# Block-sparse attention with an ELU feed-forward, one core: keys, queries and x turned on TensorE in float32, keys and rows of v in natural order, more weights loaded ahead

## The chip, the core and the metric

The kernel runs on one core of a Trainium2 chip. The core has five engines, each with its own in-order instruction queue: TensorE (PE, with its weight loads as PEld), VectorE (DVE), ScalarE (ACT), GpSimd (POOL) and SyncE (SP, which here issues DMAs). PSUM holds what TensorE writes; the other engines read it from there. The metric is the device time of one execution in microseconds. One execution was also taken with the hardware profiler, and all lines of a profile come from such an execution.

## The reference

Two parts run one after the other. Float32 q and k, v of shape (4 batches, 8 heads, 768 tokens, 64); float64 weights `w_in` (512 x 2048) and `w_out` (2048 x 512). The sequence of a batch is 24 blocks of 32 tokens.

```python
scores = scale * np.matmul(q, k.transpose(0, 1, 3, 2))
mask = np.abs(blk_i - blk_j) <= 1                       # window of three blocks
mask = mask | (blk_i == 0) | (blk_j == 0) | (blk_i == n_blocks - 1) | (blk_j == n_blocks - 1)
...                                                     # and 3 sampled key blocks per query block
scores = np.where(mask, scores, -1000000000.0)
attn = softmax(scores)                                  # max subtracted, sum + 1e-9
x = np.matmul(attn, v)        # then (4, 8, 768, 64) -> (3072 tokens, 512)
h = x @ w_in
g = np.where(h > 0.0, h, np.exp(np.minimum(h, 0.0)) - 1.0)
out = g @ w_out
```

A query block of the middle sees eight key blocks: its window of three, the first and the last, and three sampled ones. The first and the last query block see all keys.

## The kernel before, in words

**Numbers.** TensorE multiplies float16. Each float32 operand is split into a high part (ScalarE casts with a scale, `hi_part`) and a low part (VectorE subtracts, `lo_part`), and each product is three matmuls: high-high, high-low, low-high. The float64 weights are read as bits: 32 pieces of 512 KB, each made into float32 by ScalarE, VectorE and GpSimd (`w_bits1`, `w_sign`, `w_bits2`) and split (`w_split`, its low part on GpSimd at L272). The loads go through three rooms `wk`.

**Chunks.** The 22 middle blocks of a batch make five units of four blocks (128 queries) and a half unit `UL` of the last two middle blocks. With unit 5 go the first and the last block as "special" queries over all keys (the functions `sp_...`). Two units are a chunk of 256 tokens; there are twelve chunks, three per batch, the order in batch 0 being (0,1), (4,5), (2,3), later (4,5), (0,1), (2,3). The feed-forward of a chunk is 8 times `ffn_h` (192 matmuls in all, L729), the ELU on ScalarE, VectorE and GpSimd (`ffn_act1` to `ffn_act5`, L737 to L754), and 96 matmuls of `ffn_o` (L764).

**Attention of a unit**, for four heads at a time (`qd` is 0 or 1): `scores` (L534) into PSUM, softmax in float32 (`sm_min`, L545, `sm_exp`, L560), split of p (`sm_hi`, `sm_lo`, L567 and L572), a transposing DMA of p issued by SP (`sm_T`, L579), the product with v (`attn_v`, L592), and `norm` (L612). The normalised x is split on ScalarE and GpSimd (`x_hi` L619, `x_lo` L623) and turned by a transposing DMA on SP (`x_T`, L628, for unit 5 L634).

**q, k, v.** `load_kv` and `load_q` load to two staging rooms (tag "st", `NST`), SP issues. q and k are split there, high part on ScalarE (L316), low part on VectorE (L319), and turned by transposing DMAs on SP (`prep_qT` L343, `prep_kT` L366). The keys lie in `kT` with even and odd tokens apart (a block is two runs of 16), so that a window that crosses a group of 256 tokens needs two matmuls. v is split to `vN` and stored to scratch rows in DRAM (`store_v`, L449); from there come, into two tiles `vg0` and `vg1` (one for each unit of a chunk), the windows (`gather_v`, L481, two to four DMAs on SP for a block), the first and last block (`edge_v`), and the sampled blocks (one indirect DMA of GpSimd for a block, L482). The sampled keys are copied on VectorE (`gather_k`, L493).

**The first chunk** is another: batch 0's keys, queries, p and x of chunk 0 are turned on TensorE in float32 by an identity matrix (`early_k` L383, `early_q`, `early_pT` L403, `early_x` L413), four transposes to a PSUM tile, then split out of PSUM.

**Order.** Each function is put at a step with a rank (`st.at`), and the functions are run in that order. A chunk's feed-forward takes 16 steps, its attention starts `LEAD` = 22 steps before it. From this a scheduler makes the order of each engine's queue; the queues are in order, so an instruction that waits holds back all that stand behind it on its engine. Pools with a number of buffers (`NBIG`, `NT`, `NE`, `NST`) set how far loads and exponentials may run ahead.

Of the kernel before, what the change touches and what calls it, by code (L numbers as in the profile page):

```python
# [7 lines left out]
F32 = mybir.dt.float32  # L8
# [6 lines left out]
BLOCK = 32  # L15
# [23 lines left out]
def kernel(  # L39
# [35 lines left out]
    HB = BLOCK // 2  # L75
# [60 lines left out]
    def build_index():  # L136

        pk = const.tile([1, NB, 1 + NR], I32, tag="pk", name="pk")
        n = all_[0:1, :, :, 0]
        nc.vector.tensor_scalar(  # L140
            pk[:, :, 1:], n, 3, 6, op0=ALU.logical_shift_right, op1=ALU.logical_shift_left)
        nc.vector.scalar_tensor_tensor(
            pk[:, :, 1:], n, GB - 1, pk[:, :, 1:], op0=ALU.bitwise_and, op1=ALU.bitwise_or)
        nc.vector.tensor_scalar(
            pk[:, :, 0], pk[:, :, 1], 4, None, op0=ALU.logical_shift_left)
        for r in range(1, NR):
            nc.vector.scalar_tensor_tensor(
                pk[:, :, 0], pk[:, :, 1 + r], 4 + 8 * r, pk[:, :, 0],
                op0=ALU.logical_shift_left, op1=ALU.bitwise_or)
        reg[0] = pk  # L150

        pm = const.tile([P, 2], I32, tag="pm", name="pm")
        p0, p1 = pm[:, 0:1], pm[:, 1:2]
        nc.gpsimd.iota(p0, pattern=[[0, 1]], base=0, channel_multiplier=1)
        nc.vector.tensor_scalar(
            p1, p0, HB, 3, op0=ALU.bitwise_and, op1=ALU.logical_shift_left)
        nc.vector.tensor_scalar(p0, p0, HB - 1, None, op0=ALU.bitwise_and)
        nc.vector.tensor_tensor(p0, p0, p1, op=ALU.bitwise_or)
        for r in range(NR):
            ps = slice(32 * r, 32 * r + 32)  # L160
            x, n = rix[ps], all_[ps, :, r, 0]
            nc.vector.tensor_scalar(
                x, n, 3, 8, op0=ALU.logical_shift_right, op1=ALU.logical_shift_left)
            nc.vector.tensor_tensor(x, x, p0[ps].to_broadcast([32, NB]), op=ALU.bitwise_or)
            nc.vector.tensor_scalar(
                n, n, GB - 1, 4, op0=ALU.bitwise_and, op1=ALU.logical_shift_left)
# [166 lines left out]
    def prep_q_hi(b, u):
        n = q_parts(nat_tile(("q", b, u)))
        hi_part(n[:, 0], q_in(stg["q", b, u]), QS)

    def prep_q_lo(b, u):
        n = q_parts(nat["q", b, u])
        lo_part(n[:, 1], q_in(stg.pop(("q", b, u))), n[:, 0], QS)

    def prep_qT(b, u):
        qT[b, u] = work.tile([P, 2 * NPAIR, P], F16, tag="qT", name=f"qT{b}_{u}")
        nc.sync.dma_start_transpose(qT[b, u], nat.pop(("q", b, u)))  # L343

# [3 lines left out]
    def k_parts(n):  # L348

        return n.rearrange("p (c l h d) -> p l h c d", c=2, l=2, h=4)  # L350

    def prep_k_hi(b, g, qd):
        n = k_parts(nat_tile(("k", b, g, qd)))
        hi_part(n[:, 0], kv_in(stg["k", b, g, qd]), KS)

    def prep_k_lo(b, g, qd):
        n = k_parts(nat["k", b, g, qd])
        s = kv_in(stg.pop(("k", b, g, qd)))
        for c in range(2):
            lo_part(n[:, 1, :, c], s[:, :, c], n[:, 0, :, c], KS)  # L360

    def prep_kT(b, g, qd):

        if b not in kT:
            kT[b] = work.tile([P, NQ, NG, 8, P], F16, tag="kT", name=f"kT{b}")
        nc.sync.dma_start_transpose(kT[b][:, qd, g], nat.pop(("k", b, g, qd)))  # L366
# [8 lines left out]
    def early_k(g, qd):
        if 0 not in kT:
            kT[0] = work.tile([P, NQ, NG, 8, P], F16, tag="kT", name="kT0")
        s = spare(1, 2 * g, 2).rearrange("p (c x) -> p c x", c=2)
        ps = ps_f.tile([P, 2, 2, P], F32, tag="f", name=f"kt{g}_{qd}")
        for c in range(2):  # L380
            for pp in range(2):
                x = (2 * qd + pp) * P
                nc.tensor.transpose(ps[:, c, pp, :], s[:, c, x : x + P], ident)  # L383
        y = kT[0][:, qd, g].rearrange("p (c l pp) i -> p l c (pp i)", c=2, l=2)
        ps = ps.rearrange("p c pp i -> p c (pp i)")
        hi_part(y[:, 0], ps, KS)
        lo_part(y[:, 1], ps, y[:, 0], KS)

    def early_q(b, u):
        s = stg.pop(("q", b, u))  # L390
        ps = ps_f.tile([P, NPAIR, P], F32, tag="f", name=f"qt{b}_{u}")
        for pp in range(NPAIR):
            nc.tensor.transpose(ps[:, pp, :], s[:, pp * P : (pp + 1) * P], ident)
        qT[b, u] = work.tile([P, 2 * NPAIR, P], F16, tag="qT", name=f"qT{b}_{u}")
        y = qT[b, u].rearrange("p (a l) i -> p l a i", l=2)
        hi_part(y[:, 0], ps, QS)
        lo_part(y[:, 1], ps, y[:, 0], QS)

    def early_pT(b, u, qd):
# [5 lines left out]
        hi_part(y[:, 0:8], ps, PS)  # L405
        lo_part(y[:, 8:16], ps, y[:, 0:8], PS)
        pT[b, u, qd] = y

    def early_x(b, u, t, c0):
        x, s = chunk_x(t), xf.pop((b, u))  # L410
        ps = ps_s.tile([P, NPAIR, P], F32, tag="s", name=f"xt{b}_{u}")
        for cc in range(NCC):
            nc.tensor.transpose(ps[:, cc, :], s[:, cc * P : (cc + 1) * P], ident)  # L413
        cs = slice(c0, c0 + P)
        hi_part(x[:, 0, :, cs], ps, 1.0)
        lo_part(x[:, 1, :, cs], ps, x[:, 0, :, cs], 1.0)

    def keys(b, js, qd, y, k0, n):

        g, j = divmod(k0, GB)  # L420
        t = kT[b][js, qd, g].rearrange("p (c y) i -> p c y i", c=2)
        return t[:, :, y, HB * j : HB * (j + n)]

    def ends_of_k(b):

        t = work.tile([P, NQ, 4, 2, 2, HB], F16, tag="kE", bufs=1, name=f"kE{b}")
        kE[b] = t
        for e, (g, j) in enumerate(((0, 0), (NG - 1, GB - 1))):
            for qd in range(NQ):
                nc.vector.tensor_copy(  # L430
                    t[:, qd, :, e].rearrange("p y c i -> p c y i"),
                    kT[b][:, qd, g, :, HB * j : HB * j + HB].rearrange(
                        "p (c y) i -> p c y i", c=2))
# [545 lines left out]
```

## Time and profile before

| | |
|---|---|
| median of 3 runs | 880.42 us (877.14 to 887.3) |
| profiled execution | 891.87 us, its span 890.1 us |
| mean granted TensorE clock | 0.883 |
| instructions in the span | 35171 |
| DMA | 132.40 MB, mean 149 GB/s |
| GpSimd L754 (`ffn_act5`) | 114.8 us, 96 instructions |
| TensorE L729 (high part of `w_in`) | 280.9 us, 1536 matmuls |
| TensorE L764 (high part of `w_out`) | 244.1 us, 768 matmuls |

The busy shares of the engines stand in the prediction. A share is a mean over the span: it doesn't say where an engine is the bound. In a row `x22 | 24.6, 1120 | 20.6 <-ACT xn L619 20.3` the group has 22 instructions that took 24.6 us in all and 1120 ns each in the mean, and the engine stood idle for 20.6 us just before them, 20.3 of it until an instruction of ScalarE ended. Behind the row of a DMA issue on SP stand the shortest, the middle and the longest time of one, and from when to when they came.

From the first hidden matmul of a chunk to the last of its `ffn_o` the trace has: first chunk 93.8 to 211.5, second 212.3 to 290.2, third 296.1 to 354.6, ninth 683.1 to 743.0, tenth 743.9 to 795.4, twelfth 844.6 to 886.5.

### The profile page before, as it was taken

Reading aid. Unit: us, or ns where it says so; the run is one execution under the profiler, and the core shown is the slowest. Engines: PE = TensorE matmul, PEld = TensorE weight load, DVE = VectorE, ACT = ScalarE, POOL = GpSimd, SP = SyncE. Lnnn points to the kernel's source line nnn. Section 1 sums busy time; section 2 is a strip of 40 time slices with the busy share of each in tenths; the row PEclk is TensorE's granted clock in tenths of the full one; section 3 lists DMA queues with packets and bytes.
Section 4 is the critical chain, followed back from the end, with each engine's and each line's share of the span. In section 5 each row is a group of like instructions: output and inputs, shape, how many; then the busy total and the mean of one; then the engine's idle time right before and its main releaser. Section 6 shows DMA issues by size and latency. Waiting matters only on the chain.

```text
span 890.1 us, 35171 instructions
## 1 busy us (share of the span) xinstructions
PE 714.9 (80%) x15247; PEld 482.3 (54%) x15247; DVE 488.6 (55%) x1260; ACT 393.4 (44%) x826; POOL 300.5 (34%) x267
## 2 busy tenths in 40 slices
PE   3344726658698789589998897688789989999998
PEld 2233425415464665464764755555655847768483
DVE  5835679984573473446574672453544834736130
ACT  4334445643453452444553562444444634536040
POOL 1606577670142232043142430142512521523130
PEclk8555657969799999799999999799989999999999
DMA  9886998668999996667799977499759844972200
GB/s 222 212 176 163 180 204 214 171 163 174 190 183 140 184 175 145 152 130 163 126 185 179 201 153 137 107 187 156 111 103 192 167 85 93 145 156 39 49 14 24
DMA packets 263504, 132.40 MB, mean 149 GB/s; under 512 B 210612, under 2 KB 240436, under 8 KB 263348
## 3 DMA queue, kind: packets, MB, share of 16 engines
q1 hardware_dynamic: 250832, 105.68, 62.0%
q0 software_dynamic: 5632, 17.31, 8.7%
q10 hardware_dynamic: 6884, 7.15, 3.1%
q8 instruction: 119, 1.95, 1.0%
q14 instruction: 37, 0.30, 0.1%
HBM read 74.52 MB, written 12.58 MB: 98 GB/s over the span
## 4 chain that ended last, share of the span: by engine, by line
PE 47%; DMA 16%; issue 9%; SPq 8%; ACT 7%; DVE 7%; POOL 6%; DVEq 0%; POOLq 0%; ACTq 0%
PE o L764 21%; PE h L729 19%; PE s L534 4%; PE av L592 3%; DMA pT<-p 2%; DMA xT<-xn 2%; DMA spT<-spp 2%; POOL vg L482 2%; DMA wk<-in_moe_w_in_dram 2%; SPq L634 2%; DMA stk<-in_k_dram 2%; DMA stv<-in_v_dram 2%; DVE wx L262 2%; ACT t L560 2%; SPq L579 1%
## 5 line engine op out<-in xcount | busy, mean ns | idle before, releaser
L729 PE MATMUL h<-xT,wih 128*128 128x256 f16 x1536 | 280.9, 289 | 43.7 <-DVE e L747 26.5
L764 PE MATMUL o<-woh,g 128*128 128x512 f16 x768 | 244.1, 389 | 12.8 <-ACT woh L271 7.2
L754 POOL TENSOR_TENSOR g<-e,g 128x512 f16<-128x512 f32 x96 | 114.8, 1197 | 382.1 <-DVE g L751 283.9
L729 PE MATMUL h<-xT,wil 128*128 128x256 f16 x768 | 221.2, 288 | 0.0
L764 PEld LDWEIGHTS <-g 128*128 128x128 f16 x1152 | 110.8, 99 | 156.0 <-issue 34.8
L729 PEld LDWEIGHTS <-wih 128*128 128x128 f16 x1536 | 155.1, 103 | 72.6 <-issue 41.1
L764 PE MATMUL o<-wol,g 128*128 128x512 f16 x384 | 149.6, 390 | 7.5 <-POOL wol L272 5.0
L560 ACT ACTIVATE t<-t,m 128x256 f32<-128x256 f32 x176 | 87.2, 496 | 125.4 <-DVE m L545 125.4
L482 POOL DMA_INDIRECT vg<-scr,rix x88 | 89.8, 1020 | 116.1 <-PE av L592 93.6
L747 DVE SCALAR_TENSOR_TENSOR e<-h,e 128x512 f32<-128x512 f32 x96 | 66.1, 688 | 76.9 <-ACT e L743 70.7
L534 PEld LDWEIGHTS <-qT 64*32 64x32 f16 x6720 | 63.8, 92 | 79.2 <-issue 75.0
L545 DVE CUSTOM_DVE_ANT_1 t<-s,mask 128x256 f32<-128x256 f32 x176 | 64.3, 417 | 42.7 <-PE s L534 42.7
L729 PEld LDWEIGHTS <-wil 128*128 128x128 f16 x768 | 79.6, 104 | 14.9 <-issue 1.6
L534 PE MATMUL s<-kT,qT 64*32 64x96 f16 (+2 forms) x2496 | 64.1, 211 | 27.7 <-issue 11.6
L534 PE MATMUL s<-kR,qT 64*32 64x96 f16 x2112 | 68.2, 218 | 19.4 <-DVE kR L493 11.4
L737 ACT ACTIVATE e<-h 128x512 f32<-128x512 f32 x96 | 56.2, 585 | 49.3 <-PE h L729 37.6
L743 ACT ACTIVATE e<-e,gs 128x512 f32<-128x512 f32 x96 | 69.2, 721 | 2.8
L534 PE MATMUL s<-kE,qT 64*32 64x64 f16 x2112 | 63.3, 203 | 8.7 <-DVE kE L430 5.0
L572 DVE SCALAR_TENSOR_TENSOR p<-t,p 128x1024 f16<-128x1024 f32 x40 | 48.9, 1224 | 38.1 <-ACT p L567 37.8
L592 PE MATMUL av<-vg,pT 128*32 128x64 f16 x4224 | 48.4, 202 | 16.7 <-DMA pT<-p 9.8
L592 PEld LDWEIGHTS <-pT 128*32 128x32 f16 x4224 | 42.1, 98 | 35.0 <-issue 22.4
L493 DVE COPY kR<-kT 128x256 f16 x264 | 51.1, 255 | 6.0 <-issue 3.5
(103 smaller groups left out, 695.5 us busy)
## 6 DMA issues: line engine op xcount, KB each, us to landing
vg<-scr SPq DMA_DIRECT2D x144, 96.0 KB
wk<-in_moe_w_in_dram SPq DMA_DIRECT2D x16, 512.0 KB
wk<-in_moe_w_out_dram SPq DMA_DIRECT2D x16, 512.0 KB
scr<-vN SPq DMA_DIRECT2D x12, 512.0 KB
out_dram<-r ACTq DMA_DIRECT2D x20, 256.0 KB
stq<-in_q_dram SPq DMA_DIRECT2D x18, 256.0 KB
stv<-in_v_dram SPq DMA_DIRECT2D x18, 256.0 KB
stk<-in_k_dram SPq DMA_DIRECT2D x18, 256.0 KB
```

What stands on the lines that cost most here:

```text
L482: nc.gpsimd.indirect_dma_start(out=t[0:96, 1, i], out_offset=None, in_=scr[b], in_offset=bass.IndirectOffsetOnAxis(ap=rix[0:96, qb : qb + ...
L493: nc.vector.tensor_copy(t[:, :, :, c, :], kk[:, :, bass.ds(x, 7 * P + HB)].rearrange("p q (a i) -> p q a i", i=HB)[:, :, 0 :: P // HB, :])
L534: nc.tensor.matmul(oo, lhsT=qT[b, u][js, 2 * (2 * d + pp) + ql, q0 : q0 + 32], rhs=m, start=(ql + kl + part + e == 0), stop=(ql == 1), ski ...
L545: nc.vector.tensor_tensor_reduce(t[:, j, pp, :].rearrange("p (a b) -> p a b", b=BLOCK), ps[:, j, pp, :].rearrange("p (a b) -> p a b", b=BL ...
L560: nc.scalar.activation(t[:, j, pp, :], t[:, j, pp, :], AF.Exp, bias=m[:, j, pp : pp + 1], scale=-1.0, accum_out=s[:, h : h + 1])
L592: nc.tensor.matmul(o[32 * n : 32 * n + 32, 4 * qd + 2 * pp + j, :], lhsT=t[:, pl * 8 + (2 * j + pp) * 2 + ab, 32 * n : 32 * n + 32], rhs=v ...
L729: nc.tensor.matmul(ps[:, e, :], lhsT=w[2 * f + e][:, cs], rhs=x[:, l, cc, :], start=(n == 0), stop=(n == 3 * NCC - 1))
L737: nc.scalar.activation(e, hS[t, f], AF.Exp, scale=IH)
L743: nc.scalar.activation(e, e, AF.Relu, bias=gs_col, scale=-GS)
L747: nc.vector.scalar_tensor_tensor(e, hS.pop((t, f)), -IH * GS, e, op0=ALU.mult, op1=ALU.min)
L754: nc.gpsimd.tensor_tensor(gl[f], eS.pop((t, f)), gh[f], op=ALU.subtract)
L764: nc.tensor.matmul(o, lhsT=g[f][:, e, ms], rhs=w[2 * f + e], start=(f == 0 and e == 0 and n == 0), stop=(f == NFP - 1 and e == 1 and n == 2))
```

## The change

- **Keys** lie in natural order, `kT[b]` as (part, pair of heads, token). A load is 128 tokens of all heads. A window is one run of 96 tokens and needs one matmul; a block that `gather_k` copies is one run of 32; the special scores read every second token (`all_keys`).
- **Turns.** `turned` (L325 of the new kernel) makes four float32 transposes by the identity into a PSUM tile, and `split` writes the high and the low part from there. It serves all keys and queries (`turn_k`, `turn_q`) and all x (`turn_x`; unit 5's in eight quarter tiles, L363). The transposing DMAs of q, k and x, and `x_hi` and `x_lo`, are gone. p is turned as before. By the order TensorE now makes 320 float32 transposes of this kind, where there were 72; but for the first ones they share the two score buffers of PSUM with the scores.
- **v.** The scratch rows are in natural order: a window is one DMA of 96 rows, the first and last block one DMA each; batch 0's `edge_v` is issued by GpSimd.
- **Weights.** The first seven pieces are loaded at the start (`WAHEAD`), four of them into the tiles of g, which chunk 0 hasn't written yet. `NE` goes from 3 to 4 and `NST` from 2 to 3.
- **Steps.** The second chunk's attention starts 14 steps before its feed-forward where it started 22 before, and its product with v comes 4 steps after the scores and not 6.

```diff
-    NBIG, NT, NE, NST = 3, 3, 3, 2
+    NBIG, NT, NE, NST = 3, 3, 4, 3
...
+    WAHEAD = 3 + NFP // 2
+
+    def w_room(i):
+        if 3 <= i < WAHEAD:
+            g = gg[i - 3].rearrange("p a b c d -> p (a b c d)").bitcast(I32)
+            return g.rearrange("p (e w) -> p e w", w=2)
+        return wk[:, (i if i < 3 else i - WAHEAD) % 3]
...
-    def prep_kT(b, g, qd):
-
+    def turned(x, name, pool=None):
+        ps = (pool or ps_s).tile([P, 4, P], F32, tag="f" if pool else "s", name=name)
+        for a in range(4):
+            nc.tensor.transpose(ps[:, a, :], x[:, a * P : (a + 1) * P], ident)
+        return ps
+
+    def split(hi, lo, s, scale):
+        hi_part(hi, s, scale)
+        lo_part(lo, s, hi, scale)
+
+    def turn_k(b, c, pool=None):
         if b not in kT:
-            kT[b] = work.tile([P, NQ, NG, 8, P], F16, tag="kT", name=f"kT{b}")
-        nc.sync.dma_start_transpose(kT[b][:, qd, g], nat.pop(("k", b, g, qd)))
...
+            kT[b] = work.tile([P, 2, NPAIR, S], F16, tag="kT", name=f"kT{b}")
+        y = kT[b][:, :, :, c * P : (c + 1) * P]
+        split(y[:, 0], y[:, 1], turned(stg.pop(("k", b, c)), f"kt{b}_{c}", pool), KS)
+
+    def turn_q(b, u, pool=None):
+        qT[b, u] = work.tile([P, 2, NPAIR, P], F16, tag="qT", name=f"qT{b}_{u}")
+        y = qT[b, u]
+        split(y[:, 0], y[:, 1], turned(stg.pop(("q", b, u)), f"qt{b}_{u}", pool), QS)
...
+    def edge_v(b, s, eng=None):
+        for ab, s0 in ((0, 0), (1, S - BLOCK)):
+            (eng or nc.sync).dma_start(
+                vg[s][96:P, ab],
+                scr[b][s0 : s0 + BLOCK].rearrange("i (o e) -> i o e", o=1).to_broadcast(
+                    [BLOCK, QB, H * 2 * D]))
...
-        for c0, k0, n in window(qb):
-            for c in range(2):
-                p0 = c0 + HB * n * c
-                nc.sync.dma_start(t[p0 : p0 + HB * n, 0, i], v_rows(b, k0, n)[c])
+        nc.sync.dma_start(t[0:96, 0, i], scr[b][(qb - 1) * BLOCK : (qb + 2) * BLOCK])
...
-            st.at(a + 1, 1.5, lambda: x_hi(b, u))
-            st.at(a + 1, 1.6, lambda: x_lo(b, u))
-            st.at(a + 2, 0.6, lambda: x_T(b, u, t, c0))
+            st.at(a, 7, lambda: turn_x(b, u, t, c0))
...
+        elif t == 1:
+            e0 = f0 - NSTEP + 2
+            at, first = (e0, e0 + 2, e0 + 3, e0 + 5, e0 + 6), (e0, e0 + 3)
...
-        if i >= 3:
+        if i >= WAHEAD:
             st.at(s - 1, 9, lambda i=i: load_w(i))
```

What the order becomes in three places. First TensorE, in the fourth chunk's hidden matmuls (h3_4 and h3_5 are the PSUM tiles of its fifth and sixth `ffn_h`; xf1_0 is the normalised x of batch 1's unit 0, stk_2_4 the staged fifth load of batch 2's keys). Before:

```order
L729 MATMUL h3_4_7241<-xT3_5700,wih9_1914 128x256
L729 LDWEIGHTS wil9_1915
L729 MATMUL h3_4_7241<-xT3_5700,wil9_1915 128x256
L729 LDWEIGHTS wih10_1918
L729 MATMUL h3_5_7284<-xT3_5700,wih10_1918 128x256
```

And now:

```order
L629 MATMUL h3_4_7103<-xT3_5543,wih9_1482 128x256
L629 LDWEIGHTS wil9_1483
L629 MATMUL h3_4_7103<-xT3_5543,wil9_1483 128x256
L325 MATMUL xt1_0_7139<-ident_74,xf1_0_7136 128x128 x4
L325 MATMUL kt2_4_7146<-ident_74,stk_2_4_6920 128x128 x4
L629 LDWEIGHTS wih10_1486
L629 MATMUL h3_5_7153<-xT3_5543,wih10_1486 128x256
```

Two turns, eight transposes, stand between two groups of hidden matmuls, behind the last matmul of h3_4.

Next SP, at the loads of batch 1's keys and values in the second chunk's attention (stk, stv and stq are staged pieces of k, v and q, nk and xn the split k and x, scr1 the scratch rows). Before:

```order
L579 DMA_TRANSPOSE pT0_2_0_3289<-p0_2_0_3282 128x16x128
L296 DMA stk_1_0_1_3285<-in_k_dram 128x4x128
L296 DMA stv_1_1_0_3287<-in_v_dram 128x4x128
L366 DMA_TRANSPOSE kT1_3415<-nk_1_0_0_3408 128x8x128
L449 DMA scr1_3417<-vN_86 128x2x1024
L634 DMA_TRANSPOSE xT1_2518<-xn0_5_3419 128x2x64 x4
L481 DMA vg1_85<-scr0_233 48x1024
L296 DMA stk_1_1_0_3579<-in_k_dram 128x4x128
L296 DMA stv_1_1_1_3581<-in_v_dram 128x4x128
L366 DMA_TRANSPOSE kT1_3415<-nk_1_0_1_3602 128x8x128
L481 DMA vg1_85<-scr0_233 32x1024
L481 DMA vg1_85<-scr0_233 16x1024 x4
```

And now:

```order
L288 DMA stk_1_1_3199<-in_k_dram 128x8x64
L500 DMA_TRANSPOSE pT0_5_0_3056<-p0_5_0_2897 128x16x128
L500 DMA_TRANSPOSE pT0_2_0_3207<-p0_2_0_3194 128x16x128
L293 DMA stv_1_1_0_3201<-in_v_dram 128x4x128
L392 DMA scr1_3346<-vN_86 128x2048
L408 DMA vg1_85<-scr0_224 96x1024
L306 DMA stq_0_3_3203<-in_q_dram 128x8x64
L288 DMA stk_1_2_3505<-in_k_dram 128x8x64
L408 DMA vg1_85<-scr0_224 96x1024
L293 DMA stv_1_1_1_3507<-in_v_dram 128x4x128
L500 DMA_TRANSPOSE pT0_2_1_3595<-p0_2_1_3578 128x16x128
L288 DMA stk_1_3_3589<-in_k_dram 128x8x64
```

The transposes of k and x are gone, a window is one row, and what is left of transposes is p's; the loads of k and v stand between them.

Last GpSimd in the first chunk, around the gathers of the second chunk (vg0 and vg1 are its two tiles of v, wx3 and wil3 the fourth weight piece's sign and low part). Before:

```order
L482 DMA vg1_85<-scr0_233,rix_77 96x1024
L482 DMA vg0_84<-scr0_233,rix_77 96x1024
L252 TENSOR_SCALAR wx3_1288<-wk_83 128x512
L482 DMA vg0_84<-scr0_233,rix_77 96x1024 x3
L272 TENSOR_TENSOR wil3_1433<-wx3_1288,wih3_1432 128x512
L272 TENSOR_TENSOR wil4_1437<-wx4_1290,wih4_1436 128x512
```

And now:

```order
L409 DMA vg1_85<-scr0_224,rix_77 96x1024
L409 DMA vg0_84<-scr0_224,rix_77 96x1024
L244 TENSOR_SCALAR wx3_1177<-g0_79 128x512
L244 TENSOR_SCALAR wx5_1323<-g2_81 128x512
L409 DMA vg0_84<-scr0_224,rix_77 96x1024 x3
L264 TENSOR_TENSOR wil3_1315<-wx3_1177,wih3_1314 128x512
```

The first gather into vg0 stands ahead of the fourth piece's sign in both; the sixth piece's sign has moved ahead of the other three gathers, and these pieces are read from the tiles g0 and g2.

More of the change, by code (lines that the diff above doesn't have):

```diff
@@ L159, in build_index @@
+        nc.vector.tensor_scalar(pm, pm, BLOCK - 1, None, op0=ALU.bitwise_and)
         for r in range(NR):
             ps = slice(32 * r, 32 * r + 32)
[L161 to L166, printed above, removed]
@@ L375, in early_k @@
[L375 to L387, printed above, removed]
@@ L389, in early_q @@
[L389 to L399, printed above, removed]
+    def turned(x, name, pool=None):
[3 more added lines that the diff above has]
+        return ps
@@ L404, in early_pT, with turn_x @@
         y = work.tile([P, 16, P], F16, tag="pT", bufs=NT, name=f"pT{b}_{u}_{qd}")
-        hi_part(y[:, 0:8], ps, PS)
-        lo_part(y[:, 8:16], ps, y[:, 0:8], PS)
+        split(y[:, 0:8], y[:, 8:16], ps, PS)
         pT[b, u, qd] = y
-    def early_x(b, u, t, c0):
+    def turn_x(b, u, t, c0):
         x, s = chunk_x(t), xf.pop((b, u))
[L411 to L422, printed above, removed]
+        if u < UL:
+            y = x[:, :, :, c0 : c0 + P]
+            split(y[:, 0], y[:, 1], turned(s, f"xt{b}_{u}"), 1.0)
+            return
+        ps = ps_s.tile([P, NQ, 512], F32, tag="s", name=f"xt{b}_{u}")
+        for d in range(NQ):
+            ds = slice(64 * d, 64 * d + 64)
+            for pp in range(2):
+                nc.tensor.transpose(
+                    ps[:, d, 64 * pp : 64 * pp + 64], s[ds, pp * P : (pp + 1) * P], ident[ds, ds])
+        for d in range(NQ):
+            y = x[:, :, 2 * d : 2 * d + 2, c0 : c0 + 64]
+            split(y[:, 0], y[:, 1],
+                  ps[:, d, 0:P].rearrange("p (a i) -> p a i", a=2), 1.0)
     def ends_of_k(b):
-        t = work.tile([P, NQ, 4, 2, 2, HB], F16, tag="kE", bufs=1, name=f"kE{b}")
+        t = work.tile([P, 2 * NPAIR, 2, BLOCK], F16, tag="kE", bufs=1, name=f"kE{b}")
         kE[b] = t
[L428 to L433, printed above, removed]
+        for e, s0 in enumerate((0, S - BLOCK)):
+            nc.vector.tensor_copy(
+                t[:, :, e, :], kT[b].rearrange("p l a s -> p (l a) s")[:, :, s0 : s0 + BLOCK])
     def v_part(b, g, qd, l):
@@ L794, in unit @@
     def unit(s, b, u, qd, t, c0):
-        lag = 6
+        lag = 4 if t == 1 else 6
         if qd == 0:
@@ L878 @@
                 s = 2 * m
-            elif t == 1 and m == 0:
+            elif t == 2 and m == 0:
                 s += 3
             if opens:
-                st.at(s, 0.2, lambda b=b, m=m: edge_v(b, m))
+                st.at(s, 0.2, lambda b=b, m=m, e=None if t else nc.gpsimd: edge_v(b, m, e))
             for i in range(blocks_in(u)):
@@ L923 @@
     build_ident()
-    for n, (g, c) in enumerate((g, c) for g in range(NG) for c in range(2)):
-        early_k_load(g, c, (nc.sync, nc.scalar)[n % 2])
+    for c in range(NK):
+        load_k(0, c, (1, c), (nc.sync, nc.scalar)[c % 2])
     load_q(0, 0, (1, 6))
@@ L928 @@
     for n, (g, qd) in enumerate(PIECES):
-        load_kv("v", 0, g, qd, (0, n))
+        load_v(0, g, qd, (0, n))
+    for i in range(WAHEAD):
+        load_w(i)
     build_index()
     build_mask()
+    for c in range(NK):
+        turn_k(0, c, ps_f)
+    turn_q(0, 0, ps_f)
+    turn_q(0, 1, ps_f)
     for g, qd in PIECES:
-        early_k(g, qd)
-    early_q(0, 0)
-    early_q(0, 1)
-    for i in range(3):
-        load_w(i)
-    for n, (g, qd) in enumerate(PIECES):
         prep_v_hi(0, g, qd)
```

208 lines of the change are left out of this document (63 added, 145 removed).

## The prediction

> **What bounds the kernel now.** I first read the page's busy shares and DMA queues.
>
> ```profile
> PE 714.9 (80%) x15247; PEld 482.3 (54%) x15247; DVE 488.6 (55%) x1260; ACT 393.4 (44%) x826; POOL 300.5 (34%) x267
> ...
> q1 hardware_dynamic: 250832, 105.68, 62.0%
> ```
>
> TensorE leads, but 80% is a mean over stages. So next, the busy times by stretch, cut at the first chunk's first hidden matmul (93.8), its end (211.5), the end of the ninth chunk (743.5) and of the tenth (795.9), and TensorE's L729 alone in the long stretch (192 matmuls are one chunk, so 1536 are eight).
>
> ```profile
> core 0: us, PE busy (x) PEld busy (x) DVE busy (x) ACT busy (x) POOL busy (x), PEclk, DMA share, GB/s
> 0.00:93.80 93.80, 38.62 (x1388) 29.29 (x1389) 57.19 (x180) 37.64 (x84) 37.06 (x41) 0.60 0.83 192
> 93.80:211.50 117.70, 73.02 (x1199) 44.64 (x1200) 94.08 (x169) 58.79 (x111) 72.38 (x53) 0.75 0.82 189
> 211.50:743.50 532.00, 460.37 (x10149) 310.12 (x10149) 283.80 (x776) 240.73 (x518) 150.98 (x138) 0.93 0.82 154
> 743.50:795.90 52.40, 52.38 (x1320) 36.57 (x1306) 28.17 (x83) 25.55 (x58) 19.25 (x18) 1.00 0.74 129
> 795.90:890.10 94.20, 90.54 (x1246) 61.71 (x1232) 25.40 (x54) 30.65 (x57) 20.83 (x18) 1.00 0.18 38
> ```
>
> ```profile
> 211.50:743.50 532.00, 192.04 (x1536) 156.06 (x1536) 0.93 0.82 154
> ```
>
> The tenth chunk is the yardstick: 52.4 us, TensorE busy throughout, clock 1.00. Eight such chunks would be 419; the stretch took 532. So **113 us** in the middle are waits and the lower clock that follows them. The start holds the next loss: 211.5 us for one chunk. From 743.5 on TensorE alone sets the time.
>
> What are the 113 us? The chain of waits, in two places (start, us, what):
>
> ```profile
> by line: DMA pT<-p 16.6%; DMA stk<-in_k_dram 13.6%; SPq L634 6.1%; PE h L729 5.7%; ACT t L560 5.4%; DMA xT<-xn 5.1%; issue 4.9%; SPq L579 4.0%; DMA stq<-in_q_dram 3.9%; DMA kT<-nk 3.9%; SPq L481 3.4%; ACT e L737 3.3%; ACT e L743 3.2%; DVE e
> ...
> 210.21 1.27 SPq L634
> 211.53 0.57 SPq L481
> 212.22 4.37 DMA stk<-in_k_dram
> 216.70 0.63 ACT nk L316
> ```
>
> ```profile
> 667.31 6.80 DMA pT<-p
> 674.17 8.92 DMA xT<-xn
> 683.14 2.45 PE h L729 x21
> ```
>
> From 203 to 296 the chain runs through SP's queue and DMAs, hardly through TensorE. SyncE issues transposes one behind another; loads of k wait behind them; ScalarE, in order, waits for the load and holds back the exponentials of the FFN. At 667 a transpose of x lands behind a large one of p, and the hidden matmuls wait 16 us for both.
>
> **The change, part by part.**
>
> *SP's queue and the DMAs.* The issue times on SP, min/median/max in ns:
>
> ```profile
> L343 SPq DMA_TRANSPOSE qT<-nq x22: 1233/1458/3811, 34.6 to 767.9; - x22
> ...
> L366 SPq DMA_TRANSPOSE kT<-nk x18: 1231/1244/2527, 202.4 to 589.1; - x18
> ...
> L628 SPq DMA_TRANSPOSE xT<-xn x18: 1232/1254/2393, 153.5 to 837.1; - x18
> ...
> L481 SPq DMA_DIRECT2D vg<-scr x208: 302/422/1907, 37.5 to 793.1; - x104
> ```
>
> (The last row counts the DMAs.) Gone are 22 + 18 + 18 transposes and the 16 small ones of L634 (1.2 to 2 us each in the chain), some 74 x 1.3 = 96 us of SP; window gathers fall from 208 to 88, 120 x 0.42 = 50 us more. Loads of q and k stay. Of the chain from 203 to 296, L634, xT and kT go outright: 6.1 + 5.1 + 3.9 = 15%; the rest (k loads, pT) gets shorter by what stood ahead of it. So of the 113 us the least that goes is a fifth, the most all of it, since the tenth chunk still transposes p at a DMA share of 0.74 and waits for nothing. I take six tenths, **-68**: the queue loses nearly all that stands ahead of the loads, but p stays on it.
>
> [...]
>
> *TensorE's price.* A turn is four float32 transposes; before has 72 matmuls of this kind, after 320 by the order. Their price, and the clock there:
>
> ```profile
> 13.77 0.88 PE L383 MATMUL kt<-ident,vg 128*128 128x128 f32 x6 [1.15 <-DMA vg<-in_k_dram]
> ```
>
> ```profile
> 34.21 1.94 PE L403 MATMUL pt<-ident,t 128*128 128x128 f32 x8
> ```
>
> ```profile
> 13.70:14.70 1.00, 0.88 (x6) 0.64 (x6) 0.00 (x0) 0.00 (x0) 0.00 (x0) 1.00 1.07 234
> 34.20:36.20 2.00, 1.95 (x11) 1.65 (x9) 1.55 (x6) 2.00 (x7) 1.43 (x2) 0.50 0.65 158
> ```
>
> 0.88/6 = 0.15 us at the full clock, 1.94/8 = 0.24 at half, tails included. Of the 248 added, 32 stand before the second chunk's matmuls, where TensorE idles anyway; 216 x 0.15 = 32 us, of which the remaining waits (45 of 532) cover about a tenth. Scores lose 384 matmuls, as windows no longer split:
>
> ```profile
> 334.90 1.30 PE s L534 x140
> ```
>
> 384 x 1.30/140 = -3.6. I take **+24** (15 to 52).
>
> *New waits of TensorE.* It now waits itself for a load (k, q), for the normalised x, and for one of two score buffers in PSUM. Where a turn follows its input directly, the row is
>
> ```profile
> 71.52 1.12 PE L413 MATMUL xt<-ident,xf 128*128 128x128 f32 x4 [0.96 <-DVE xf L612]
> ```
>
> In the order a group of FFN matmuls (2.5 to 5 us) mostly stands between. 62 added turns; I take 0.2 us each, **+12**; ends 0 and 62 x 0.96 = 60. Queued behind a blocked turn are all later matmuls, so this is the price to watch.
>
> *ScalarE, VectorE, GpSimd.*
>
> ```profile
> L623 POOL TENSOR_TENSOR xn<-xf,xn 128x512 f16<-128x512 f32 (+1 forms) x22 | 24.6, 1120 | 20.6 <-ACT xn L619 20.3
> ...
> L319 DVE SCALAR_TENSOR_TENSOR kT<-kt,kT 128x512 f16<-128x512 f32 x6 | 4.1, 689 | 4.7 <-ACT kT L316 4.5
> ```
>
> x's low part moves from POOL (1.1 us) to VectorE (0.69 from PSUM, as for the keys above); q's is read from PSUM too. Sums change by a few us on engines about half busy: nothing. Random keys are copied in runs of 32 instead of 16 elements, and the special scores read keys two apart; no row shows either form; by their present busy times I bound each by half, up or down, and take zero.
>
> *The start.* Weight pieces end with a subtraction on POOL:
>
> ```profile
> 70.83 0.92 POOL L482 DMA_INDIRECT vg<-scr,rix  x1 [26.80 <-PE av L592]
> 71.77 1.56 POOL L252 TENSOR_SCALAR wx<-wk 128x512 f32<-128x512 f32 x1
> ```
>
> ```profile
> L272 POOL TENSOR_TENSOR wil<-wx,wih x16: 1154/1164/1663, 38.4 to 130.7; 128x512 f16<-128x512 f32 x16
> ```
>
> ```profile
> L272 POOL TENSOR_TENSOR wol<-wx,woh x16: 1144/1184/1610, 133.5 to 199.6; 128x512 f16<-128x512 f32 x16
> ```
>
> The last 16 come every (199.6 - 133.5)/15 = 4.4 us; POOL's own work is 1.2 plus half of 1.6, so loading through three rooms paces them. POOL stands 27 us before the second chunk's gather, which waits for the first chunk's product with v; in the new order that gather still stands ahead of piece 3's sign, so this block stays. But seven pieces (four more at once, three issued ahead of the next windows) lie ready when it ends: 7 x (4.4 - 2.2) = **-15**, with 2.2 for POOL's and VectorE's work on a piece. Ends: 0, as the four loads now stand ahead of the store of v, and -39, where VectorE (94 of 118 us busy) would be full. The move of the second chunk's attention costs nothing if the weights hide it, as they do now; else its chain of p is late, about a transpose of 7 us each.
>
> **Sum.** The profiled execution took 891.87 us, span 890.1. -68 + 24 + 12 - 15 = -47: 845. The median of the runs shown, 880.42, is 0.987 of the profiled time, so **834**.
>
> **Rivals.**
>
> 1. *All the middle's waits go* (the tenth chunk's state throughout): -113 + 24 + 0 - 20 = -109, 783, or **773**. For: that chunk transposes p, x and q and waits for nothing. Against: it loads no keys.
> 2. *Little goes*: p's transposes, k and v loads still pace the middle. -23 + 24 + 6 - 10 = -3: 889, or **877**. For: pT is 16.6% of that chain and stays.
> 3. *Slower: TensorE blocked by its turns.* A late k or q load used to block ScalarE; now it blocks the matmuls directly. It decides above 59/62 = 0.95 us a turn (the other terms sum to -59). At 2.2 us (half the 4.37 us load above): -47 + 62 x 2.0 = +77: 969, or **956**. Against: the order puts other matmuls between, and three rooms replace two.
> [...]
>
> **Chances.** Forecast 0.50, first rival 0.20, second 0.15, third 0.08, fourth 0.07. Under 1% is what a measurement cannot tell from no change; the second rival lies there or just beside it, so it goes to "same" for two thirds, the rest to both sides: faster 0.77 + 0.03 = 0.80, same 0.10, slower 0.08 + 0.02 = 0.10. The range reaches from the first rival to the second: 772 to 878; beyond it lie the third and what goes further than the first and the second.
>
> **What would show it.** In the profile after: the eight chunks' stretch near 490 us, with a clock above 0.95; no load of k or q in the chain for more than a few us; waits of TensorE's turns under 15 us in all; the last piece of w_out split near 185; DMA share of the middle still about 0.8. I am wrong if turns wait over 1 us each, or if pT's DMAs fill the chain as before.

## The result and the profile after

The changed kernel took **852.66 us** (median of 4 runs, 850.52 to 854.58), the kernel before 883.86 (4 runs, 877.14 to 890.38) beside it: ratio **0.967**, 95% interval 0.959 to 0.975. A second set of runs (experiment e9 below) gave 0.959 (0.954 to 0.965). The medians of the kernel before in the four sets of this case were 883.9, 885.5, 888.7 and 894.6 us (the three later sets each on another chip), so a time is compared below by its ratio to the kernel before in its own set, and two kernels of one set directly.

The profiled execution took 850.52 us, span 848.8, clock 0.925. Its page first: busy shares and the queue that SP issues to.

```profile
PE 716.1 (84%) x15111; PEld 497.2 (59%) x15111; DVE 473.2 (56%) x1247; ACT 390.9 (46%) x830; POOL 270.5 (32%) x249
...
q1 hardware_dynamic: 191952, 88.89, 50.1%
```

TensorE's busy time is what it was (714.9 before), in 41 us less. Cut at the same places as before (first hidden matmul of the first chunk, its end, end of the ninth chunk, of the tenth), by stretch:

```profile
core 0: us, PE busy (x) PEld busy (x) DVE busy (x) ACT busy (x) POOL busy (x), PEclk, DMA share, GB/s
0.00:76.30 76.30, 31.67 (x1043) 25.62 (x1044) 46.09 (x145) 32.09 (x70) 29.82 (x39) 0.76 0.93 239
76.30:201.50 125.20, 79.88 (x1515) 50.81 (x1514) 105.54 (x194) 66.62 (x134) 76.13 (x57) 0.77 0.68 170
201.50:697.20 495.70, 459.33 (x10074) 320.33 (x10073) 266.16 (x767) 235.49 (x512) 129.38 (x122) 0.97 0.66 137
697.20:752.30 55.10, 54.05 (x1260) 37.87 (x1248) 28.18 (x86) 25.56 (x59) 16.67 (x16) 1.00 0.55 108
752.30:848.80 96.50, 91.19 (x1257) 62.57 (x1256) 27.25 (x57) 31.16 (x58) 18.52 (x16) 1.00 0.17 32
```

The first chunk ends at 201.5 instead of 211.5 (-10): its hidden matmuls begin at 76.3 instead of 93.8, but it then takes 125.2 us instead of 117.7. The eight chunks of the middle take 495.7 instead of 532.0 (-36). The last three take 151.6 instead of 146.6 (+5). In the middle, the stretch of those eight chunks, TensorE is busy as long as before (459.3 and 460.4), but it waits 36.4 us instead of 71.6, at a clock of 0.97 instead of 0.93. The equal busy time hides two changes: the turns are new, and all else got shorter. The turns in the middle, at L325 and unit 5's at L363:

```profile
201.50:697.20 495.70, 28.80 (x184) 22.42 (x183) 0.97 0.66 137
...
201.50:697.20 495.70, 1.02 (x12) 0.61 (x12) 0.97 0.66 137
```

Whom TensorE waits for in the middle, before and then after (total, times, longest):

```profile
PE h L729 <- DVE e L747: 20.0, 4, 5.7
```

```profile
PE xt L325 <- DVE xf L533: 11.8, 5, 6.9
PE kt L325 <- ACT spt L567: 7.8, 2, 4.9
PE h L629 <- issue: 7.5, 4, 3.3
```

Before, hidden matmuls waited for PSUM buffers that the ELU chain (e, L747) gave back late. That wait is gone from the head of the list. In its place stand turns of x behind the normalisation (`xf`), and turns of k that wait for a score buffer held by the special scores (`spt`): with one turn at 0.3, together 19.9 us. The loads of k, with who waited for them, now:

```profile
L288 SPq DMA_DIRECT2D stk<-in_k_dram x18: 367/389/1518, 100.0 to 533.7; - x18
...
  ACT spt L567: 15.8, 4
  issue: 1.1, 2
  DVE xT L316: 0.8, 2
...
DMA to landing us min/median/max: 2.9/3.6/10.3
```

No turn waits for a landing load of later batches' keys: of what the view lists, none is that DMA. (The chain of this profile reaches back only to 653, so it can't say what paced the middle.)

### The profile page after: what moved, and what is told of

It is laid out like the page before. It is cut to its first block, busy times and chain, and to the rows that moved or that the text cites. A ratio compares the mean times of both kernels' runs of the same rounds, so it can differ in the third digit from the quotient of the medians.

```text
span 848.8 us, 34525 instructions
## 1 busy us (share of the span) xinstructions
PE 716.1 (84%) x15111; PEld 497.2 (59%) x15111; DVE 473.2 (56%) x1247; ACT 390.9 (46%) x830; POOL 270.5 (32%) x249
## 5 line engine op out<-in xcount | busy, mean ns | idle before, releaser
L629 PE MATMUL h<-xT,wih 128*128 128x256 f16 x1536 | 271.4, 282 | 16.3 <-issue 6.2
L664 PE MATMUL o<-woh,g 128*128 128x512 f16 x768 | 242.1, 383 | 5.6 <-ACT woh L263 3.6
L629 PE MATMUL h<-xT,wil 128*128 128x256 f16 x768 | 216.3, 282 | 3.1 <-issue 3.1
L664 PEld LDWEIGHTS <-g 128*128 128x128 f16 x1152 | 109.5, 98 | 139.2 <-issue 19.3
L629 PEld LDWEIGHTS <-wih 128*128 128x128 f16 x1536 | 151.5, 101 | 41.5 <-issue 17.5
L664 PE MATMUL o<-wol,g 128*128 128x512 f16 x384 | 147.2, 383 | 6.7 <-POOL wol L264 5.6
L409 POOL DMA_INDIRECT vg<-scr,rix x88 | 84.4, 959 | 133.6 <-PE av L513 113.7
L455 PEld LDWEIGHTS <-qT 64*32 64x32 f16 x6336 | 56.5, 91 | 57.1 <-issue 43.5
L629 PEld LDWEIGHTS <-wil 128*128 128x128 f16 x768 | 77.6, 101 | 16.0 <-POOL wx L244 3.1
L455 PE MATMUL s<-kE,qT 64*32 64x64 f16 x2112 | 57.4, 201 | 15.0 <-issue 11.9
L455 PE MATMUL s<-kR,qT 64*32 64x96 f16 x2112 | 60.8, 215 | 9.3 <-issue 6.7
L455 PE MATMUL s<-kT,qT 64*32 64x96 f16 x2112 | 56.5, 216 | 14.4 <-DVE m L466 10.0
L513 PEld LDWEIGHTS <-pT 128*32 128x32 f16 x4224 | 42.6, 98 | 18.7 <-issue 16.2
```

Of the source, the lines that this page charges most:

```text
L409: nc.gpsimd.indirect_dma_start(out=t[0:96, 1, i], out_offset=None, in_=scr[b], in_offset=bass.IndirectOffsetOnAxis(ap=rix[0:96, qb : qb + ...
L455: nc.tensor.matmul(o, lhsT=qT[b, u][js, ql, a, q0 : q0 + 32], rhs=m, start=(ql + kl + part == 0), stop=(ql == 1), skip_group_check=True)
L513: nc.tensor.matmul(o[32 * n : 32 * n + 32, 4 * qd + 2 * pp + j, :], lhsT=t[:, pl * 8 + (2 * j + pp) * 2 + ab, 32 * n : 32 * n + 32], rhs=v ...
L629: nc.tensor.matmul(ps[:, e, :], lhsT=w[2 * f + e][:, cs], rhs=x[:, l, cc, :], start=(n == 0), stop=(n == 3 * NCC - 1))
L664: nc.tensor.matmul(o, lhsT=g[f][:, e, ms], rhs=w[2 * f + e], start=(f == 0 and e == 0 and n == 0), stop=(f == NFP - 1 and e == 1 and n == 2))
```

## The experiments

**Rooms.** e1 takes back only the pools:

```diff
-    NBIG, NT, NE, NST = 3, 3, 4, 3
+    NBIG, NT, NE, NST = 3, 3, 3, 2
```

> The changed kernel with the exponential rooms back from 4 to 3 and the staging rooms from 3 to 2; all else stays. My theory: the gain comes from the transposing DMAs and window DMAs that left SP's queue; the rooms carry little of it: 850 to 860 us. Rival (the third staging room lets loads of k, q and v run ahead, and that is the gain): 870 us or more.

Measured: 865.72 us, ratio 0.980 (0.972 to 0.988). The changed kernel's two ratios are 0.967 and 0.959, so the rooms carry 1.3 to 2.1%, some 12 to 18 us of 885 (each ratio is known to 0.8%): more than my theory allowed, less than the rival. In e1's trace the first chunk ends at 208.6, against 201.5 in the changed kernel and 205.3 in its second trace (e9), and the middle takes 499.2, against 495.7 and 499.3. So at most 3.5 us of what the rooms give is seen in the middle. The profiled executions of e1 and e9 differ by 2 us only (862.77 and 860.85), so where the rest lies is not shown.

**All transposes back.** e2 brings back the tile `nat` for the split inputs and stands on e1, whose pools are the smaller ones; e1 is what it is compared with.

```diff
-        st.at(s, 7.2, lambda: turn_k(b, c))
+        st.at(s, 3.6, lambda: dma_k(b, c))
+        st.at(s + 1, 0.7, lambda: dma_kT(b, c))
```

`dma_k` splits the loaded keys on ScalarE and VectorE, `dma_kT` turns them by a transposing DMA on SP. (q and x in the same way, x's low part on GpSimd, at the steps of the kernel before.)

> The kernel of e1_pools with later batches' keys, all queries behind the first chunk's and all x behind the first chunk's split in natural order and turned by transposing DMAs on SP again, at the steps of the kernel before; natural order and single-DMA windows stay. My theory: the transposes are the cause, so most of the middle's 36 us come back, the part of the windows stays gained: 870 to 885 us, with load and transposes in the chain. Rival (the windows, 88 DMAs for 208, are the cause): within 1% of e1_pools.

Measured: 897.39 us, 31.7 more than e1 in the same set (runs 896.6 to 898.0 against 862.8 to 873.1), and 1.3% slower than the kernel before. That is over the 870 to 885 of my theory: nothing of the gain is left, not even a part of the windows. So what carries it is that the transposing DMAs left, with the splits that stood ahead of them, and not the windows. By stretch (start, middle, end):

```profile
0.00:210.80 210.80, 109.41 (x2543) 73.24 (x2546) 156.00 (x338) 98.84 (x204) 111.07 (x97) 0.74 0.78 195
210.80:737.00 526.20, 454.81 (x9849) 307.32 (x9848) 274.34 (x746) 236.99 (x509) 152.62 (x138) 0.94 0.81 154
737.00:894.90 157.90, 145.17 (x2496) 99.21 (x2496) 52.92 (x137) 56.87 (x114) 40.12 (x36) 0.98 0.36 66
```

The middle is back to 526.2, with 71.4 us of waits and a clock of 0.94: nearly the picture before. But for the rooms, all the rest of the change is in e2, so this is the plainest evidence for the cause. The waits of TensorE in it are again the old ones:

```profile
PE h L674 <- DVE e L692: 27.1, 10, 7.1
PE h L674 <- DMA xT<-xn: 9.3, 7, 3.3
```

The end is 11.3 us longer than before (157.9 against 146.6), though the same transposes stand there. What of the new order costs that, once transposes are back on SP, was not found.

**Which input.** e11 and e12 put only x, and only the later batches' k, back on SP (again on e1, which ran in another set). q alone was not tried.

> The kernel of e1 with x alone behind the first chunk turned by DMAs again (18 large and 16 small transposes on SP), k and q on TensorE. e2, all three by DMA, was 31.7 us over e1. My theory (what counts is the time the transposes take of SP's queue, ahead of loads): x's share of it, 51 of 140 us in e2's rows, makes 31.7 x 51/140 = 12 us over e1's 865.7. Rival (x's transposes stand straight in the path to the hidden matmuls, 9.3 us of waits in e2, so x carries most): 20 us or more over e1. Other rival (x's turns cost TensorE as much in waits as the DMAs did): within 5 us of e1.

> The kernel of e1 with later batches' keys alone turned by DMAs again (18 transposes on SP, and k split by ScalarE behind a waited load), q and x on TensorE. My theory, by SP's time: 25 of 140 us, so 6 us over e1's 865.7. Rival (a wait of ScalarE for a late load of k, in order ahead of the exponentials, is the main cause, as the chain from 203 to 296 of the kernel before looked): 15 us or more over e1.

Measured: x alone 887.56 us, ratio 0.992 (0.988 to 0.996), 1.1% or 10 us over e1's ratio, near the 12 of SP's time; the two intervals leave 2 to 18. k alone **900.43 us**, ratio 1.008 (1.005 to 1.012), 2.8% or 25 us over e1, where SP's time said 6; in one set it is 12.9 us over x alone. k alone costs nearly what all three cost; the rival for k holds. Its trace shows a path. ScalarE and VectorE on the staged keys, and for whom they stood idle:

```profile
L313 ACT ACTIVATE nk<-stk x18: 612/632/632, 170.1 to 564.3; 128x512 f16<-128x512 f32 x18
L316 DVE SCALAR_TENSOR_TENSOR nk<-stk,nk x18: 678/693/1405, 189.0 to 564.9; 128x512 f16<-128x512 f32 x18
its engine sat idle before it (us, times) until:
  DMA stk<-in_k_dram: 63.2, 15
  ACT nk L313: 50.4, 15
```

ScalarE waits 63.2 us for 15 loads of k; VectorE, in order behind it, waits 50.4 us for ScalarE. And then TensorE, in the middle, for them:

```profile
PE xt L325 <- DVE xf L578: 30.0, 6, 8.2
PE xt L325 <- ACT e L682: 9.4, 3, 4.1
...
PE xt L408 <- DVE xf L578: 7.7, 2, 4.1
```

Together 47.1 us, where e1's middle has 16.3:

```profile
PE xt L325 <- DVE xf L533: 15.3, 5, 6.8
...
PE xt L363 <- DVE xf L533: 1.0, 1, 1.0
```

The normalisation of x stands in VectorE's queue behind the low part of k (at 340 and at 537 directly: k's at 340.05 and 537.42, x's at 340.66 and 538.02), and a turn of x (L325, unit 5's at L408) blocks TensorE until it comes. At the longest wait, 8.2 us until 379, a split of v that waits for its own load stands between, too. So in e12 what a transposing DMA of k costs is not its own time on SP but that its input is split by ScalarE and VectorE straight off the load. e12 also puts that split at an earlier rank (3.6) than the turn has (7.2); whether a split at 7.2 would wait less was not tried.

That this was the path in the kernel before, too, is not shown: behind the first chunk no turn of x could block TensorE there. By its profile the splits of k waited 16.7 us for loads of k; the splits of q waited longer, for transposes of x:

```profile
  DMA xT<-xn: 34.8, 4
```

The split x, k and q share the two rooms of the tile `nat`, so a split of k or q can also wait until a transpose of x has freed one. For both together the profiles have 42.1 us of that before and 54.4 in e2. e11 and e12, which each bring back one input, don't have this wait, so their prices need not add up to e2's. e2 less e11, across sets, leaves 2.2% or 19 us for k and q where x goes by DMA.

**The price of a turn.**

```diff
-        for a in range(4):
+        for a in [0, 1, 2, 3] * (1 if pool else 2):
             nc.tensor.transpose(ps[:, a, :], x[:, a * P : (a + 1) * P], ident)
```

> The changed kernel with every turn of k, q and x behind the start made twice into the same PSUM tile (four transposes more each, 52 turns). The row of these transposes in the changed kernel's profile says 28.8 us for 184 in the middle, 0.157 each. My theory: TensorE is the bound there, the price shows nearly in full: 208 x 0.157 = +33, 880 to 888 us. Rival (the waits that remain, 36 us in the middle, hide turns): +10 or less, under 863 us.

Measured: 871.18 us, ratio 0.983 (0.976 to 0.990), 1.6 to 2.3% over the changed kernel's ratios: 14 to 21 us for 208 transposes, 0.07 to 0.10 us each, between theory and rival. In the trace the second transposes, whose input is already there, cost less than the first: 0.115 us where those of the changed kernel take 0.157. The row of L325 in e3's middle, and the stretch itself:

```profile
208.90:716.50 507.60, 49.20 (x362) 43.43 (x361) 0.98 0.63 134
...
208.90:716.50 507.60, 475.61 (x10215) 338.10 (x10213) 262.15 (x761) 237.33 (x510) 130.61 (x122) 0.98 0.63 134
```

(49.20 - 28.80) / (362 - 184) = 0.115 us each, where the changed kernel's rows give 28.80 / 184 = 0.157. That the difference is the tail of a group, which a group of eight has only once, is my reading: with 0.273, the median of one, 3 x 0.115 + 0.273 = 0.62, and a group of four takes 0.60 in the changed kernel's trace (at 303.70).

**The start.** e4 loads three pieces ahead, not seven; e8 keeps pieces 3 to 8 off GpSimd.

```diff
-    WAHEAD = 3 + NFP // 2
+    WAHEAD = 3
```

> The changed kernel with three weight pieces loaded ahead as before, not seven. My theory (loading through three rooms paced the pieces): the first chunk's end moves back by the 10 us that it gained, 201.5 to 211: 858 to 866 us. Rival (VectorE paces the pieces, 105.5 of 125.2 us busy in the first chunk): no change, 849 to 857 us.

Measured: 858.43 us, ratio 0.970 (0.963 to 0.976), 0.3 to 1.0% over the changed kernel (2 to 9 us); the first chunk ends at 210.7. The first chunk's end moves back by the start's gain in the trace, though in the time the interval holds no change too. The first hidden matmul stays at 76.2, so the pieces loaded ahead shorten the chunk (134.5 us here), and don't bring it earlier.

```diff
+    WE = 6
...
-        if i % 2:
+        if i % 2 and not 3 <= i < 3 + WE:
             nc.gpsimd.tensor_scalar(
...
-        nc.gpsimd.tensor_tensor(lo[f], x, hi[f], op=ALU.subtract)
+        (nc.vector if 3 <= i < 3 + WE else nc.gpsimd).tensor_tensor(lo[f], x, hi[f], op=ALU.subtract)
```

> The changed kernel with the sign and the low part of weight pieces 3 to 8 made on VectorE and not on GpSimd, so that none of them stands behind GpSimd's gather for the second chunk, which waits for the first chunk's product with v. My theory (that block costs the start): the first chunk ends 8 to 15 us earlier than 201.5, 838 to 846 us. Rival (VectorE, 105.5 of 125.2 us busy in the first chunk, paces the pieces with or without the block): no change or some us slower, 850 to 860 us.

Measured: 850.90 us, ratio 0.957 (0.954 to 0.960); the first chunk ends at 206.2, no earlier than in the changed kernel (201.5, and 205.3 in e9). The low parts of the weights in e8:

```profile
L266 DVE TENSOR_TENSOR wil<-wx,wih x6: 672/678/1127, 73.3 to 85.6; 128x512 f16<-128x512 f32 x6
L266 POOL TENSOR_TENSOR wol<-wx,woh x16: 1143/1270/2132, 112.2 to 187.3; 128x512 f16<-128x512 f32 x16
```

Off GpSimd, the six pieces still come only from 73.3 on, and the last piece of w_out comes at 187.3 (187.6 in the changed kernel). GpSimd's block doesn't set the start; my theory fell. What the last sixteen wait for, 5.0 us a piece, stays open between the rooms and VectorE.

**The second chunk's steps, the windows, the turns of x.**

> The changed kernel with the second chunk's attention at the steps of the kernel before (22 steps ahead of its feed-forward, product with v 6 steps behind the scores). My theory: the weights hide where it stands: within 1%, 847 to 860 us. Rival (the move lets the weight pieces of the first chunk pass ahead of the second chunk's softmax on VectorE, and is a part of the start's gain): the first chunk ends 5 to 15 us later, 858 to 868 us.

Measured: 854.98 us, ratio 0.961 (0.958 to 0.964): between the changed kernel's two, so no effect on the time, as the theory had it. The rival's sign came in small: the first hidden matmul comes at 83.4 and the first chunk ends at 207.1 (205.3 and 201.5 in the changed kernel's traces).

```diff
-        nc.sync.dma_start(t[0:96, 0, i], scr[b][(qb - 1) * BLOCK : (qb + 2) * BLOCK])
+        for w in range(3):
+            nc.sync.dma_start(
+                t[32 * w : 32 * w + 32, 0, i], scr[b][(qb - 1 + w) * BLOCK : (qb + w) * BLOCK])
```

> The changed kernel with each window of 96 rows of v fetched by three DMAs of 32 rows: 264 DMAs on SP instead of 88, the same bytes. At 0.42 us an issue that is 176 x 0.42 = 74 us of SP's time, spread over 790 us. My theory (SP's queue matters only where slow transposes stand in it): within 1%, 848 to 861 us. Rival (the single window DMA is a large part of the gain): 865 us or more.

Measured: 846.46 us, ratio 0.953 (0.949 to 0.957). Three times as many issues cost nothing. The rows of the window DMAs in the changed kernel and in e6 (min/median/max of an issue in ns):

```profile
L408 SPq DMA_DIRECT2D vg<-scr x88: 303/422/6040, 32.0 to 742.8; - x88
```

```profile
L409 SPq DMA_DIRECT2D vg<-scr x264: 302/420/3150, 31.7 to 740.3; - x132
```

An issue takes the same 0.42 us, so SP does 74 us more, and no engine but TensorE's weight loads (0.3 us) waits for them.

```diff
-            st.at(a, 7, lambda: turn_x(b, u, t, c0))
+            st.at(a + 1, 7, lambda: turn_x(b, u, t, c0))
```

> The changed kernel with the turns of x one step later, so that a group of feed-forward matmuls stands between the normalisation and the turn. In the changed kernel's profile turns of x wait 11.8 us for the normalised x in the middle. My theory (a wait of TensorE costs its full length): 8 to 12 us less, 841 to 846 us. Rival (the wait is made up behind it, or the next consumer is late instead): 849 to 856 us.

Measured: 846.15 us, ratio 0.952 (0.949 to 0.955). TensorE's waits for the normalised x fall, in the whole span, from

```profile
PE xt L325 <- DVE xf L533: 18.1, 7, 6.9
```

to

```profile
PE xt L325 <- DVE xf L533: 4.6, 2, 2.4
```

e6 and e7 look 0.6 to 1.5% faster than the changed kernel, but that was timed in other sets. So it was run again beside the two together:

> The changed kernel once more, as it is, beside the other three on one chip. The kernel before took 883.9, 885.5 and 888.7 us in the medians of three sets of runs, so small differences between sets can't be read; this run says where the changed kernel lies beside the variants. Expected by both theories: ratio to before 0.960 to 0.970.

> The changed kernel with the edits of e6 and e7 together: windows by three DMAs, turns of x one step later. My theory (the two take away different waits: e7 turns' waits for the normalised x, e6 work of the first two chunks in another order and later DMAs): both gains add, 836 to 843 us, ratio 0.940 to 0.950. Rival (both shift the same slack): as e7 alone, ratio 0.950 to 0.955.

Measured: the changed kernel 858.66 us (853.4 to 860.9), ratio 0.959 (0.954 to 0.965), a hair under what was expected; both edits together 856.86 (851.0 to 859.5), ratio 0.957 (0.951 to 0.963). The runs overlap. My theory fell, and the middle value lies beside the rival's range, too: together the edits give no gain that can be measured. In e10 the waits of x's turns are 4.6 us as in e7, 16 us under the 20.6 of e9; yet all of TensorE's waits in the whole span fall by 8 only, from 133.2 us to 125.1, and hidden matmuls wait 15.9 us for the ELU chain (e) where they waited 6.5. So the wait of a turn is in good part replaced by other waits, and no version is shown here to beat the changed kernel.

## Why the prediction held, and where it was off

**The time.** 834 was forecast, in 772 to 878; 852.66 came, a gain of 3.3% (4.1% in the second set) where 5.3% was forecast. In the profiled execution itself the sum was close: 845 against 850.5, the middle near 490 against 495.7, the clock there above 0.95 against 0.97, the last piece of w_out near 185 against 187.6. Some of that closeness is luck: it is the fastest of its four runs. The second trace of the same kernel (e9, an execution of 860.85 us) leaves 16 us:

```profile
0.00:205.30 205.30, 114.44 (x2557) 77.02 (x2558) 152.49 (x338) 98.92 (x204) 105.14 (x95) 0.73 0.76 193
205.30:704.60 499.30, 459.66 (x10034) 320.50 (x10033) 267.34 (x766) 234.87 (x510) 128.87 (x122) 0.97 0.64 136
704.60:859.10 154.50, 147.44 (x2524) 101.87 (x2522) 55.58 (x143) 57.47 (x116) 35.16 (x32) 0.99 0.30 58
```

**The step that failed most is the last one**, the factor 0.987 from the profiled time to the median. It took the profiled execution (891.87) as slow beside a median of three runs (880.42). With a fourth run that set's median is 883.9, and the later sets have 885.5 to 894.6: 891.87 was an ordinary time, and 880.42 a low one. Of the 18.7 us between 834 and 852.66, 5.5 are in the terms by the first trace (845 against 850.5); the other 13 come from this factor.

**SP's queue and the DMAs, -68.** By the traces, waits in the middle fell from 71.6 to 36.4, of which 19.9 are new: 55 us of old waits went. With the better clock (0.97 for 0.93) the feed-forward's matmuls of the middle got shorter. The busy time of the hidden ones fell from 192.04 to 185.05 us, that of `ffn_o` from 179.37 to 174.85 (L764 before; L629 and L664 after):

```profile
211.50:743.50 532.00, 179.37 (x769) 73.79 (x768) 0.93 0.82 154
```

```profile
201.50:697.20 495.70, 185.05 (x1536) 151.60 (x1536) 0.97 0.66 137
```

```profile
201.50:697.20 495.70, 174.85 (x769) 71.91 (x768) 0.97 0.66 137
```

That is 55 + 11.5 = 67 us: the size was right. Its reason was right in part only. The prediction reckoned in SP's time, 96 us of transposes and 50 us of windows. e6 shows that the windows' issues are worth nothing, and e11 and e12 that SP's time is a poor measure of the worth of a transpose: 25 us of SP's time for k was worth 25 us, 51 us for x was worth about 10. What e12 shows at work is the other half of that paragraph, ScalarE in order behind a load; how much of it was in the kernel before is not shown, as the shared rooms `nat` held its splits back, too. And the sum had no term for the rooms (NE, NST), 12 to 18 us by e1; at most 3.5 of them are in the middle's gain.

One of the two places in the chain was misread. At 667 the hidden matmuls didn't wait 16 us for the transposes of p and x: the chain there is that of the ninth chunk's first matmul, and TensorE was busy with other work nearly throughout. In the whole middle its hidden matmuls waited 4.6 us for a turned x.

```profile
667.30:683.10 15.80, 15.68 (x410) 8.20 (x409) 8.95 (x25) 6.58 (x16) 5.14 (x5) 1.00 1.05 178
```

```profile
PE h L729 <- DMA xT<-xn: 4.6, 2, 3.9
```

**How fast transposing DMAs land.** In e2 they land about as fast as loads: the medians are 4.1 us for k, 4.5 for q and 3.2 for x (16 of whose 34 are small), against 3.5 for a load of k and 6.0 for one of q.

```profile
stk<-in_k_dram SPq DMA_DIRECT2D x18, 256.0 KB, 3.5
...
xT<-xn SPq DMA_TRANSPOSE x34, 3.2
...
qT<-nq SPq DMA_TRANSPOSE x22, 4.5
kT<-nk SPq DMA_TRANSPOSE x18, 4.1
```

So it isn't by late landings of their own that they cost: e2 gives back 31.7 us with transposes that land that fast.

**TensorE's price, +24.** e3 puts 14 to 21 us on 208 transposes; the term for 216 was 32 less a cover of a tenth. The rate, 0.15 with tails, was too high by a third beside the 0.115 of e3's second transposes. 208 of those would be 24 us, so 12 to 41% of the price is covered by waits, where a tenth was taken. The scores fell by 8.8 us in the middle alone (busy 50.91 to 42.10), where 3.6 was taken for all; some of that may be the clock (0.97 for 0.93).

**New waits of turns, +12.** 19.9 us in the middle, 0.4 us for each of its 49 turns where 0.2 was taken; the test "under 15 us in all" failed. The price is softer than its length: e7 and e10 take most of x's share away, and e10 shows no gain beside e9. The buffer of PSUM that was named only in passing is 7.8 of the 19.9.

**The start, -15.** -10 in the trace (-6 in e9's); e4 ties 2 to 9 us of it to the pieces loaded ahead, and e1's 208.6 leaves room for a part by the rooms, which the term didn't have. The working with GpSimd's block fell in e8. Nor did the last sixteen pieces come faster: one every (187.6 - 116.2)/15 = 4.8 us, where it was 4.4. They began earlier, with the whole first chunk: 17.5 us, of which e5 ties 5 to 7 to the second chunk's steps, and the rest stays open. (The end of -39 doesn't follow from its row: 117.7 less 94.1 us leaves 24 until VectorE is full.)

**Taken at zero:** the second chunk's steps (e5: right for the time). The special scores with keys two apart took 383 ns by the median where they took 376, the copies of `gather_k` 221 where 218: right too.

```profile
L549 PE MATMUL sp<-kT,qT x192: 270/383/632, 106.8 to 648.0; 64*64 64x512 f16 x96, 64*64 64x256 f16 x96
```

**The rivals.** Not all waits went (36.4 stay), and not little went. *TensorE blocked by its turns* didn't come: no turn waits for a load of k, and 19.9 us over the middle's 49 turns is 0.4, under the 0.95 that would have decided. The fourth, *the clock*, was an estimate: were the clock at half under the turns, 216 transposes at 0.24 us instead of 0.15 would add 19 us, so 853. That is the very time that came, but not by this way: the middle's clock rose from 0.93 to 0.97 with the turns and stood at 0.98 with twice as many (e3), and a transpose's median in the middle of the changed kernel is 273 ns, where those of p take 421, at a clock of 0.50 in four of their five stretches (36.7 to 63.8 us). At 49 us of them among 476 us of TensorE's work in e3 no loss of clock can be seen; no run shows a turn that lowers it. The DMA share was expected to stay at 0.8 and fell to 0.66: the transposes that left make the difference, as e2's 0.81 beside e1's 0.65 shows.

## What to carry to other kernels

When a load's first reader is an in-order engine that also serves the main chain, a late load can hold that chain back (in e12 ScalarE stood idle 63.2 us for loads of k, and TensorE in the middle 47.1 us for what came behind it); look for the engine's waits on DMAs, and don't price a DMA by its issue time or its bytes alone. Handing the load to an engine whose queue places the reading later, here TensorE with a turn between feed-forward groups, can be worth more than the operation it adds: k by DMA was 25 us slower in e12, and 72 transposes at e3's 0.115 us are 8. A wait on a load isn't a price, either: the changed kernel's ScalarE still waits 39.8 us in the middle for loads of v, and what that costs was not tried. Rooms that two inputs share tie their queues together: in `nat` the splits of k and q waited 42.1 us for transposes of x before, 54.4 in e2. An added operation can be priced by doing it twice, as e3 did: 14 to 21 us for 208 transposes.

## What was not expected of the hardware

The same kernel's medians differ by 1.2% between sets of runs (883.9 to 894.6; whether the chip or something else of a set makes it is not shown), more than several of the effects that were looked for; e6 and e7, read across sets, looked like gains of 6 us and more that e10 beside e9 did not confirm. Float32 transposes of 128 x 128 behind others of their kind go at 0.115 us each at a clock of 0.98 (e3), though a single one's time is 0.273 us by the median in the changed kernel's middle. Tripling the DMAs of the windows (88 to 264) changed no issue time (422 ns by the median, then 420), and the median landing went from 5.9 us for 192 KB to 3.9 us for 64 KB.
